# Dates for each chunk and each tile, written out as lists, in a planned kernel of attention and two mixtures

## The chip, the cores and the metric

The kernel runs on one core of a Trainium2 chip. The metric is the time of one execution on the device, in microseconds (us). Of three runs of the kernel before the median is 1030.25 us (1030.01 to 1031.8).

## The reference, cut to what matters

```python
# gated linear attention: 4 batches x 8 heads x 768 steps x 48
for t in range(S):
    state = alpha[:, :, t, :, None] * state + einsum('bhd,bhe->bhde', k[:, :, t], v[:, :, t])
    y[:, :, t] = einsum('bhd,bhde->bhe', q[:, :, t], state)
x = y.transpose(0, 2, 1, 3).reshape(3072, 384)

# first mixture, d_ff = 2048
h = x @ w_in
P = a[0] + a[1] * h + a[2] * h**2 + a[3] * h**3
Q = 1.0 + abs(b[0]) * abs(h) + abs(b[1]) * h**2
x = (P / (Q + 1e-06)) @ w_out

# second mixture, d_ff = 1536
g = x @ w_gate
out = (g * sigmoid(g) * (x @ w_val)) @ w_out
```

All arrays are float32 (weights may come as float64, which the kernel reads as pairs of words).

## The kernel before, in words

**Three stages.** Attention is worked in 24 chunks of 128 steps (`attention`, six for each batch): four transposes and products on TensorE, two scans and two products on VectorE (L669, L677, L685, L695), copies on ScalarE, masks on GpSimd. Its result goes through DRAM (`xd`) to the first mixture. The first mixture (`moe1`) works in six blocks of 512 tokens and 16 slices of 128 of d_ff; one slice of one block is a *tile*. A tile is nine multiplications into `h` (`mm1`), then a chain on ScalarE, GpSimd and VectorE that evaluates P / Q (L866 to L896, L880 and L807 on GpSimd, L881 to L892 on VectorE), and nine multiplications (`mm2`) into three accumulators `acc`. Every product is made of three, from values split into a rounded part and its rest. The second mixture (`moe2`) does the same with `pg`, `pv` and four accumulators `po`. Beside them every weight is brought in and split (`split`: ScalarE, VectorE, GpSimd), and in the end `bounds` reads alpha and the weights again and counts values out of range.

**Segments.** The spec given to `segments` cuts the first mixture into nine runs of tiles, each of one block: block 0, slices 0 to 5; block 1, 0 to 5; block 2, 0 to 5; block 3, all; block 0, 6 to 15; block 1, 6 to 15; block 2, 6 to 15; block 4, all; block 5, all. After the last tile of each, the three accumulators are emptied to `ys` (L921 on ScalarE, or, for the second part of a block, L927 on VectorE, added to what the first part left in DRAM), and `ys` is stored to `y1d`, from where the second mixture reads it. The next segment's `mm2` needs the accumulators' banks; there are three of them. Tiles of the next segment can run their `mm1` before that, as far as the other five banks and the four buffers of `gg` go.

**The planner.** `plan.op(v, how, reads, writes)` notes a step with a date v, its engine (or several, in order of preference) and a duration. `order` first works out when each step is due, from the last to the first:

```python
t = [due[u] - (dur + self.hop(e, ...) if full else 0.0) for u, full in users[i]]
if e == PE or not t:
    t.append(v)
due[i] = min(t)
...
due = [d - self.bias.get(g, 0.0) for d, g in zip(due, self.groups)]
```

`users` are the steps that depend on this one. So a step on TensorE is due at its own date or when its users need it; any other step goes by its users, and by its own date only if it has none. Then the planner goes through time with the durations it was given. Where an engine is free, it takes, of the steps that are ready on it, the one that is due first; it doesn't wait for a date. A step's second engine may be taken only from `due + late - THETA` on, where `late` is how far TensorE's last step was behind its due time. The order in which steps were picked is the order of the instructions in each engine's queue, and of the loads and stores in SP's queue.

**The dates.** `cv[m]` is the date of chunk m, whose steps on TensorE are dated up to 6 x 1.28 behind it. `vs` holds, for each segment, the date of each tile's `mm1`; its `mm2` is dated MM2 behind it. Before the change both come from formulas: a tile takes `step` (4.08), and the chunks' need is spread over the tiles at PA = 7.58 each. `vs2` are the dates of the second mixture's tiles, P2 apart; its `mm4` is dated 9.09 behind. The biases set the chunks ("att"), the weights ("w"), the loads of x ("x") and the tiles ("moe") against each other.

Of the kernel before, what the change touches and what calls it, by code (L numbers as in the profile page):

```python
# [19 lines left out]
PE, DVE, ACT, POOL, DMA = range(5)  # L20
CAPS = {"w": 99, "early": 9, "att": 3, "h": 5, "acc": 3, "po": 4, "g": 4, "tr": 1, "cv": 1}
HOP = {PE: 0.22, DVE: 0.2, ACT: 0.2, POOL: 0.15, DMA: 2.1}
SAME = {PE: 0.0, DVE: 0.07, ACT: 0.09, POOL: 0.05, DMA: 2.1}
THETA = 3.82


class Buf:
# [327 lines left out]
def gla_moe_moe2_kernel(  # L355
# [18 lines left out]
    NT, DM = out.shape  # L374
    F1 = w_in.shape[1] // 128
    F2 = w_gate.shape[1] // 128
    C = 128
# [6 lines left out]
    SIZES = [512,512,512,512,512,512]  # L384
    TMAX = max(SIZES)
    HEAD = [sum(SIZES[:n]) for n in range(len(SIZES) + 1)]
# [7 lines left out]
    plan = Plan()  # L394
# [68 lines left out]
    for nm in "akqv":  # L463
        for i in range(NBV if nm == "v" else 1):
            t = A.tile([128, H, 64], F32, name=f"nat{nm}{i}")
# [336 lines left out]
    def pool(T, f):  # L802
        return (POOL, 0.2 + T * 0.0021, f)
# [37 lines left out]
    def moe1(vs, n, part, f0, f1, xt, win, wout):  # L841
        acc = [bank("acc", f"acc{j}") for j in range(NJ)]

        T = SIZES[n]

        def first(f):
            v = vs[f - f0]
            hb = bank("h", "h")

            def h():  # L850
                return hb.t[:, 0:T]

            def cut(b):
                return lambda: b.t[:, 0:T]

            def mm1():
                for j in range(NJ):
                    s = slice(j * 128, (j + 1) * 128)
                    x = xt[j].t
                    mm3(h(), win[f].t[:, 0, s], win[f].t[:, 1, s], x[:, 0, 0:T], x[:, 1, 0:T], j == 0, j == NJ - 1)  # L860

            plan.op(v, [(PE, 9 * (T / 2400 + 0.0135), mm1)], (win[f], *xt, params), (hb,))
            b1, b2, b4 = (new("mp", [128, TMAX], F32, x, c) for x, c in (("t1", 3), ("t2", 2), ("t4", 3)))
            t1, t2, t4 = cut(b1), cut(b2), cut(b4)
            gg = new("mp", [128, 2, TMAX], F32R, "gg", LAG + 1)
            plan.op(v, [act(T, lambda: nc.scalar.activation(t1(), h(), AF.Abs), sb=False)], (hb,), (b1,))  # L866
            plan.op(
                v,
                [
                    act(T, lambda: nc.scalar.activation(  # L870
                        t2(), t1(), AF.Identity, scale=absb[:, 1:2], bias=absb[:, 0:1]), 2),
                    (POOL, 0.17 + T * 0.001, lambda: nc.gpsimd.tensor_scalar(
                        t2(), t1(), absb[:, 1:2], absb[:, 0:1], ALU.mult, ALU.add)),
                ],
                (b1,), (b2,),
            )
            plan.op(v, [act(T, lambda: nc.scalar.activation(t4(), h(), AF.Identity, scale=a3, bias=a2), 2, False)],
                    (hb,), (b4,))

            plan.op(v, [pool(T, lambda: nc.gpsimd.tensor_tensor(t1(), t1(), t2(), ALU.mult))], (b1, b2), (b1,))  # L880
            plan.op(v, [dve(T, lambda: nc.vector.tensor_tensor(t4(), t4(), h(), ALU.mult))], (b4, hb), (b4,))  # L881
            plan.op(v, [dve(T, lambda: nc.vector.scalar_tensor_tensor(t4(), t4(), a1, h(), ALU.add, ALU.mult), 1)],
                    (b4, hb), (b4,))
            plan.op(v, [act(T, lambda: nc.scalar.activation(t2(), t1(), AF.Ln, bias=oneps), 1)], (b1,), (b2,))
            last_exp[0] = plan.op(v, [act(T, lambda: nc.scalar.activation(h(), t2(), AF.Exp, scale=-1.0))], (b2,), (hb,))  # L885
            plan.op(v, [dve(T, lambda: nc.vector.scalar_tensor_tensor(t1(), t1(), ONE_EPS, h(), ALU.add, ALU.mult))],  # L886
                    (b1, hb), (b1,))
            plan.op(v, [dve(T, lambda: nc.vector.scalar_tensor_tensor(h(), t4(), a0, h(), ALU.add, ALU.mult), 1)],
                    (b4, hb), (hb,))
            plan.op(  # L890
                v,
                [dve(T, lambda: nc.vector.scalar_tensor_tensor(  # L892
                    t4(), t1(), 2.0, h(), ALU.subtract, ALU.mult, reverse0=True))],
                (b1, hb), (b4,),
            )
            plan.op(v, [act(T, lambda: nc.scalar.copy(gg.t[:, 0, 0:T], t4()))], (b4,), (gg,))  # L896
            plan.op(v, sub(T, lambda: gg.t[:, 1, 0:T], t4, lambda: gg.t[:, 0, 0:T])[:1], (b4, gg), (gg,))
            return gg

        def second(f, gg):  # L900
            def mm2():
                for j in range(NJ):
                    s = slice(j * 128, (j + 1) * 128)
                    w, g = wout[f].t, gg.t
                    mm3(acc[j].t[:, 0:T], w[:, 0, s], w[:, 1, s], g[:, 0, 0:T], g[:, 1, 0:T], f == f0, f == f1 - 1)

            plan.op(vs[f - f0] + MM2, [(PE, 9 * (T / 2400 + 0.0135), mm2)], (wout[f], gg), tuple(acc))

        pend = []
        for f in range(f0, f1):  # L910
            pend.append((f, first(f)))
            if len(pend) > LAG:
                second(*pend.pop(0))
        for z in pend:
            second(*z)
        vl = vs[-1] + MM2
        for j in range(NJ):
            ys = new("mp", [128, TMAX], F32, "ys", YS)
            yc = cut_(ys, T)
            if part == 0:  # L920
                how = [act(T, lambda j=j, yc=yc: nc.scalar.copy(yc(), acc[j].t[:, 0:T]), 0, False),  # L921
                       dve(T, lambda j=j, yc=yc: nc.vector.tensor_copy(yc(), acc[j].t[:, 0:T]))]
                plan.op(vl - 2.0, how, (acc[j],), (ys,))
            else:
                plan.op(vl - 8.0, [(DMA, 0.6 * T / 384, lambda j=j, yc=yc: nc.sync.dma_start(yc(), y1d[n].t[j]))],
                        (y1d[n],), (ys,))
                how = [dve(T, lambda j=j, yc=yc: nc.vector.tensor_tensor(yc(), yc(), acc[j].t[:, 0:T], ALU.add))]  # L927
                plan.op(vl - 2.0, how, (acc[j], ys), (ys,))
            plan.op(vl - 6.0, [(DMA, 0.6 * T / 384, lambda j=j, yc=yc: nc.sync.dma_start(y1d[n].t[j], yc()))],
                    (ys,), (y1d[n],))  # L930

# [97 lines left out]
    def moe2(vs, n, f0, f1, yy, wg, wv, wo):  # L1029
        po = [bank("po", f"po{t}") for t in range(CPB)]  # L1030
# [27 lines left out]
        def second(f, pp):  # L1058
            def mm4():
                for t in range(CPB):  # L1060
                    s = slice(t * 128, (t + 1) * 128)
                    o, w = po[t].t[:, 0:DM], wo[f].t
                    nc.tensor.matmul(o, pp.t[:, 0, s], w[:, 0], start=f == f0, stop=False)  # L1063
                    nc.tensor.matmul(o, pp.t[:, 0, s], w[:, 1], start=False, stop=False)  # L1064
                    nc.tensor.matmul(o, pp.t[:, 1, s], w[:, 0], start=False, stop=f == f1 - 1)  # L1065

            plan.op(vs[f - f0] + 9.09, [(PE, 2.09, mm4)], (wo[f], pp), tuple(po))

        pend = []
        for f in range(f0, f1):  # L1070
# [5 lines left out]
        vl = vs[-1] + 4.0  # L1076
# [26 lines left out]
            plan.op(vl, [(DMA, 0.6, lambda os=os, r0=r0: nc.sync.dma_start(out[r0 : r0 + 128, :], os.t))], (os,), ())  # L1103


    PA, P2 = 7.58, 6.18
    MM2 = 16.91

    def segments(nf, spec):

# [6 lines left out]
        return r  # L1117

    segs = segments(F1, "0:0-6 1:0-6 2:0-6 3 0:6-16 1:6-16 2:6-16 4 5")
    step = [18 * (SIZES[n] / 2400 + 0.0135) for n, _, _, _ in segs]  # L1120

    at, need = [0.0], []
    for (n, part, f0, f1), p in zip(segs, step):
        need.append((at[-1], HEAD[n + 1] // C if part == 0 else 0))
        at.append(at[-1] + p * (f1 - f0))
    s0 = 36.82
    LEADM = 53.00
    done = HEAD[1] / C
    cv = [3.50 + 6.65 * m for m in range(HEAD[1] // C)]
    start, vs = [], []  # L1130
    t, w = s0, 0.0
    for (n, part, f0, f1), p in zip(segs, step):
        start.append(t)
        row = []
        for f in range(f0, f1):
            row.append(t)
            rate = max([(k_ - done) / max(w_ - w - LEADM, p) for w_, k_ in need if w_ > w and k_ > done], default=0.0)
            c = min(rate * p, NT / C - done)
            while len(cv) < int(done + c + 1e-6):
                cv.append(max(t - 16.20, cv[-1] + 5.80))  # L1140
            done += c
            w += p
            t += p + PA * c
        vs.append(row)
    end_a = t
    i0 = len(plan.ops)
    plan.bias = {"w": -4.22, "att": 12.04, "x": 0.54, "moe": -2.25}
    plan.group = "att"
    for m in range(NT // C):
        if m == 1:  # L1150
# [13 lines left out]
    plan.group = None  # L1164

    segs2 = segments(F2, "0:0-2 1:0-2 2:0-2 0:2-6 1:2-6 2:2-6 0:6-12 1:6-12 2:6-12 3 4 5")
    t, vs2 = end_a + 16.75, []
    for n, part, f0, f1 in segs2:
        vs2.append([t + P2 * i for i in range(f1 - f0)])
        t += P2 * (f1 - f0)  # L1170
    wg, wv, wo = [], [], []
# [4 lines left out]
        wo.append(load_f(vw + 3.0, "wo", w_out2, f))  # L1176
    for (n, part, f0, f1), row in zip(segs2, vs2):
        moe2(row, n, f0, f1, load_y(row[0], n), wg, wv, wo)
    flag = bounds(end_a + 94.88, vs2[-1][0] - 20.0)

    for _, i, f in plan.order():
        for b in plan.ops[i][3]:
# [43 lines left out]
```

## Time and profile before

| | us |
|---|---|
| median of three runs (lowest, highest) | 1030.25 (1030.01, 1031.8) |
| the profiled execution | 1031.37 |
| its span, first to last instruction | 1029.7 |
| TensorE busy (matmul) | 993.9 |
| TensorE busy (weight load) | 836.6 |
| VectorE busy | 766.4 |
| ScalarE busy | 612.7 |
| GpSimd busy | 466.4 |

The mean granted clock of TensorE was 0.99. In the trace, PE is TensorE, PEld its loading of weights, DVE VectorE, ACT ScalarE, POOL GpSimd, SP the engine whose queue issues the loads and stores. In brackets at the end of a row of the timeline stands how long the engine had been idle before it, and what ended that. Names such as `h`, `acc`, `gg`, `ys`, `aT`, `pp` are those of the code. A matmul is shown with its time from entry to end; the next enters before that, so the pace of TensorE is read from the starts.

### The profile page before, as it was taken

To read this page: it belongs to the slowest core of one execution; us is meant where nothing else is said; L and a number is where in the kernel's file an instruction comes from. 1 tells how busy PE (TensorE), PEld (TensorE's weight loads), DVE (VectorE), ACT (ScalarE), POOL (GpSimd) and SP (SyncE) were. 2 spreads that over 40 slices of the span, in tenths; PEclk is the share of its full clock that TensorE was granted. 3 is DMA by queue.
4 is the path that set the end of the run, shared out by engine and by line. 5 is a ranking of instruction groups with operands and counts; after the bars stand their busy time and mean duration, and the time that the engine had idled before them with its cause. 6 is when DMAs were issued, how large, how long until landed. Compare 5 with 4: busy or idle time off the path is not lost.

```text
span 1029.7 us, 15684 instructions
## 1 busy us (share of the span) xinstructions
PE 993.9 (97%) x5542; PEld 836.6 (81%) x5542; DVE 766.4 (74%) x1442; ACT 612.7 (60%) x1120; POOL 466.4 (45%) x433
## 2 busy tenths in 40 slices
PE   8899999999999999999899999999999999999997
PEld 7777787778888788878678888888888888888886
DVE  6999988898869968797879784369876666666322
ACT  4676899899988868889989673222222112212111
POOL 2348887998856756666989883000000000000000
PEclk9999999999999999999989999999999999999999
DMA  7888754434322221220132661133653543543000
GB/s 169 202 194 203 194 140 131 131 101 108 93 72 54 90 63 48 71 91 1 32 108 77 195 204 47 46 108 108 192 175 110 183 122 114 154 123 96 28 1 34
DMA packets 159462, 113.56 MB, mean 110 GB/s; under 512 B 105232, under 2 KB 132880, under 8 KB 159376
## 3 DMA queue, kind: packets, MB, share of 16 engines
q1 hardware_dynamic: 159376, 112.49, 39.6%
q8 instruction: 45, 0.74, 0.3%
q14 instruction: 41, 0.34, 0.1%
HBM read 95.95 MB, written 16.52 MB: 109 GB/s over the span
## 4 chain that ended last, share of the span: by engine, by line
PE 46%; ACT 3%; DVE 2%; POOL 1%; issue 1%; DMA 0%; DVEq 0%; SPq 0%; POOLq 0%
PE pv L837 5%; PE pv L839 5%; PE pv L838 5%; PE pg L838 5%; PE pg L839 5%; PE po L1065 5%; PE po L1063 5%; PE po L1064 5%; PE pg L837 5%; PE acc L837 1%; PE acc L839 1%; PE acc L838 1%; PE h L837 1%; PE h L838 1%; PE h L839 1%
## 5 line engine op out<-in xcount | busy, mean ns | idle before, releaser
L880 POOL TENSOR_TENSOR t<-t,t 128x512 f32<-128x512 f32 x96 | 125.2, 1305 | 48.0 <-ACT t L870 41.0
L807 POOL TENSOR_TENSOR gg<-t,gg 128x512 fp32r<-128x512 f32 x96 | 128.8, 1343 | 39.7 <-ACT gg L896 21.9
L1046 ACT ACTIVATE sg<-pg 128x512 f32<-128x512 f32 x72 | 43.1, 598 | 170.7 <-PE pg L839 170.0
L1047 DVE TENSOR_TENSOR sg<-sg,pv 128x512 f32<-128x512 f32 x72 | 49.5, 687 | 126.5 <-PE pv L839 126.5
L837 PE MATMUL h<-xt,win 128*128 128x512 f32 x288 | 117.0, 406 | 13.5 <-DVE t L892 8.7
L1049 ACT CAST pp<-sg 128x512 fp32r<-128x512 f32 x72 | 44.8, 622 | 131.8 <-DVE sg L1047 118.9
L837 PE MATMUL acc<-gg,wout 128*128 128x512 f32 x288 | 115.5, 401 | 2.0 <-DVE t L892 2.0
L839 PE MATMUL h<-xt,win 128*128 128x512 f32 x288 | 114.0, 396 | 0.3 <-DVE win L530 0.3
L838 PE MATMUL h<-xt,win 128*128 128x512 f32 x288 | 114.0, 396 | 0.0
L838 PE MATMUL acc<-gg,wout 128*128 128x512 f32 x288 | 113.2, 393 | 0.3 <-POOL gg L807 0.2
L839 PE MATMUL acc<-gg,wout 128*128 128x512 f32 x288 | 112.7, 391 | 0.0
L886 DVE SCALAR_TENSOR_TENSOR t<-t,h 128x512 f32<-128x512 f32 x96 | 65.4, 683 | 46.9 <-ACT h L885 45.7
L1063 PE MATMUL po<-wo,pp 128*128 128x384 f32 x288 | 97.2, 337 | 0.7 <-ACT part L1087 0.7
L1065 PE MATMUL po<-wo,pp 128*128 128x384 f32 x288 | 97.2, 338 | 0.0
L1064 PE MATMUL po<-wo,pp 128*128 128x384 f32 x288 | 96.9, 337 | 0.0
L838 PE MATMUL pg<-yy,wg 128*128 128x512 f32 x216 | 85.1, 394 | 0.7 <-DVE yy L945 0.7
L837 PE MATMUL pv<-yy,wv 128*128 128x512 f32 x216 | 85.6, 396 | 0.0
L839 PE MATMUL pv<-yy,wv 128*128 128x512 f32 x216 | 85.4, 395 | 0.0
L838 PE MATMUL pv<-yy,wv 128*128 128x512 f32 x216 | 85.2, 395 | 0.0
L839 PE MATMUL pg<-yy,wg 128*128 128x512 f32 x216 | 85.2, 394 | 0.0
L837 PE MATMUL pg<-yy,wg 128*128 128x512 f32 x216 | 84.9, 393 | 0.0
L981 DVE TENSOR_SCALAR_CACHE_REDUCE chk_x<-chk_e 128x384 f32<-128x384 uint32 x136 | 75.1, 552 | 3.8
(143 smaller groups left out, 2492.2 us busy)
## 6 DMA issues: line engine op xcount, KB each, us to landing
chk<-in_moe_w_out_dram SPq DMA_DIRECT2D x28, 384.0 KB, 3.3
yr<-y1d SPq DMA_DIRECT2D x36, 256.0 KB, 2.7
xr<-xd SPq DMA_DIRECT2D x27, 256.0 KB, 2.8
y1d<-ys SPq DMA_DIRECT2D x27, 256.0 KB, 2.3
win_st<-in_moe_w_in_dram SPq DMA_DIRECT2D x16, 384.0 KB, 3.8
wout_st<-in_moe_w_out_dram SPq DMA_DIRECT2D x16, 384.0 KB, 3.8
chk<-in_moe_w_in_dram SPq DMA_DIRECT2D x16, 384.0 KB, 3.9
nata<-in_alpha_dram SPq DMA_DIRECT2D x24, 192.0 KB, 3.4
```

The lines of the kernel that those rows point to most:

```text
L807: return lambda: eng.tensor_tensor(out_(), in0(), in1().bitcast(F32), ALU.subtract)
L837: nc.tensor.matmul(out_, wh, xh, start=start, stop=False)
L838: nc.tensor.matmul(out_, wh, xl, start=False, stop=False)
L839: nc.tensor.matmul(out_, wl, xh, start=False, stop=stop)
L880: plan.op(v, [pool(T, lambda: nc.gpsimd.tensor_tensor(t1(), t1(), t2(), ALU.mult))], (b1, b2), (b1,))
L886: plan.op(v, [dve(T, lambda: nc.vector.scalar_tensor_tensor(t1(), t1(), ONE_EPS, h(), ALU.add, ALU.mult))], (b1, hb), (b1,))
L981: [(DVE, 0.4, lambda: nc.vector.tensor_scalar(dst(), src(), bound, 0.0, op_, ALU.add, accum_out=cnt.t[:, c : c + 1]))],
L1047: plan.op(v, [(DVE, 0.6, lambda: nc.vector.tensor_tensor(sg.t, sg.t, pv.t, ALU.mult))], (sg, pv), (sg,))
L1049: plan.op(v, [(ACT, 0.53, lambda: nc.scalar.copy(pp.t[:, 0], sg.t))], (sg,), (pp,))
L1063: nc.tensor.matmul(o, pp.t[:, 0, s], w[:, 0], start=f == f0, stop=False)
L1064: nc.tensor.matmul(o, pp.t[:, 0, s], w[:, 1], start=False, stop=False)
L1065: nc.tensor.matmul(o, pp.t[:, 1, s], w[:, 0], start=False, stop=f == f1 - 1)
```

## The change

The formulas for the dates of chunks and tiles go, and two lists stand in their place. THETA, three biases, P2, MM2, the second mixture's start, the dates of `mm4`, of the emptying copies and of the checks get other numbers. No step, no size and no buffer is changed.

```diff
-THETA = 3.82
+THETA = 3.39
...
-                plan.op(vl - 2.0, how, (acc[j],), (ys,))
+                plan.op(vl - EV, how, (acc[j],), (ys,))
...
-                plan.op(vl - 2.0, how, (acc[j], ys), (ys,))
+                plan.op(vl - EV, how, (acc[j], ys), (ys,))
...
-            plan.op(vs[f - f0] + 9.09, [(PE, 2.09, mm4)], (wo[f], pp), tuple(po))
+            plan.op(vs[f - f0] + 9.60, [(PE, 2.09, mm4)], (wo[f], pp), tuple(po))
...
-    PA, P2 = 7.58, 6.18
-    MM2 = 16.91
+    MM2 = 16.92
+    EV = 5.79
...
-    s0 = 36.82
-    LEADM = 53.00
-    done = HEAD[1] / C
-    cv = [3.50 + 6.65 * m for m in range(HEAD[1] // C)]
...
-            rate = max([(k_ - done) / max(w_ - w - LEADM, p) for w_, k_ in need if w_ > w and k_ > done], default=0.0)
-            c = min(rate * p, NT / C - done)
-            while len(cv) < int(done + c + 1e-6):
-                cv.append(max(t - 16.20, cv[-1] + 5.80))
-            done += c
-            w += p
-            t += p + PA * c
-        vs.append(row)
-    end_a = t
+    cv = [3.5, 10.6, 17.0, 27.5, 29.5, 33.6, 40.7, 46.8, 52.0, 54.8, 66.1, 64.2, 93.7, 105.3, 115.4, 125.5, 162.8, 209.7, 250.2, 293.5, 328.7, 371.3, 413.4, 460.2]
+    vs = [
+        [36.3, 100.0, 113.2, 124.8, 136.4, 148.0],
+        [152.2, 157.3, 163.9, 167.4, 172.5, 177.5],
+        [182.6, 187.7, 192.7, 197.3, 202.3, 201.8],
+        [212.5, 217.5, 222.6, 227.7, 232.7, 238.3, 243.3, 248.4, 253.5, 258.5, 263.6, 268.7, 272.3, 277.4, 282.5, 287.5],
+        [294.0, 299.0, 304.1, 308.5, 314.2, 319.3, 324.4, 336.1, 341.2, 346.2],
+        [351.3, 356.4, 361.4, 366.5, 365.7, 371.5, 376.6, 381.7, 386.8, 391.8],
+        [396.8, 401.9, 407.0, 409.9, 416.1, 421.2, 419.4, 426.6, 431.6, 433.9],
+        [441.0, 446.0, 451.1, 456.6, 460.3, 464.3, 469.3, 473.4, 477.5, 480.7, 484.8, 488.8, 492.9, 497.0, 501.1, 505.2],
+        [509.3, 513.3, 515.0, 523.5, 527.6, 531.7, 535.8, 539.8, 543.9, 549.8, 551.8, 555.6, 559.2, 561.9, 564.9, 569.4],
+    ]
+    P2 = 6.45
+    end_a = 585.14
...
-    plan.bias = {"w": -4.22, "att": 12.04, "x": 0.54, "moe": -2.25}
+    plan.bias = {"w": -3.37, "att": 12.90, "x": 0.25, "moe": -2.25}
...
-    t, vs2 = end_a + 16.75, []
+    t, vs2 = end_a + 5.14, []
...
-    flag = bounds(end_a + 94.88, vs2[-1][0] - 20.0)
+    flag = bounds(end_a + 103.59, vs2[-1][0] - 20.0)
```

## Rows read from the trace of the kernel before

**Rows 1.** The page, part 1: busy us, share of the span, instructions.

```profile
PE 993.9 (97%) x5542; PEld 836.6 (81%) x5542; DVE 766.4 (74%) x1442; ACT 612.7 (60%) x1120; POOL 466.4 (45%) x433
```

**Rows 2.** Busy us of each engine in stretches of the span.

```profile
core 0: us, PE busy (x) PEld busy (x) DVE busy (x) ACT busy (x) POOL busy (x), PEclk, DMA share, GB/s
60.00:80.00 20.00, 17.88 (x168) 14.11 (x167) 19.93 (x35) 16.45 (x35) 11.39 (x12) 1.00 0.77 177
...
280.00:300.00 20.00, 20.00 (x131) 16.19 (x129) 13.87 (x22) 16.96 (x31) 11.08 (x10) 1.00 0.25 73
...
380.00:400.00 20.00, 20.00 (x130) 16.37 (x129) 14.91 (x24) 17.07 (x31) 12.85 (x13) 1.00 0.36 107
...
680.00:740.00 60.00, 60.00 (x289) 52.23 (x288) 55.58 (x157) 13.88 (x23) 0.00 (x0) 1.00 0.53 160
```

**Rows 3.** TensorE's timeline at five changes of segment: start, us.

```profile
181.71 0.50 PE L837 MATMUL h<-xt,win 128*128 128x512 f32 x1 [2.65 <-ACT al L662]
...
183.22 0.60 PE L837 MATMUL h<-xt,win 128*128 128x512 f32 x1
...
186.66 0.40 PE L839 MATMUL acc<-gg,wout 128*128 128x512 f32 x1
...
211.58 0.50 PE L837 MATMUL h<-xt,win 128*128 128x512 f32 x1 [1.53 <-DVE qt L695]
...
346.93 0.69 PE L837 MATMUL h<-xt,win 128*128 128x512 f32 x1 [2.53 <-DVE t L892]
...
350.68 0.39 PE L837 MATMUL acc<-gg,wout 128*128 128x512 f32 x1
...
447.62 0.50 PE L837 MATMUL acc<-gg,wout 128*128 128x512 f32 x1 [2.02 <-DVE t L892]
...
517.23 0.80 PE L837 MATMUL h<-xt,win 128*128 128x512 f32 x1 [6.21 <-DVE t L892]
...
521.21 0.39 PE L837 MATMUL acc<-gg,wout 128*128 128x512 f32 x1
```

**Rows 4.** The timelines of GpSimd and TensorE at the last product of block 4.

```profile
496.67 1.30 POOL L807 TENSOR_TENSOR gg<-t,gg 128x512 fp32r<-128x512 f32 x1
...
498.29 0.39 PE L837 MATMUL h<-xt,win 128*128 128x512 f32 x1
...
500.33 0.39 PE L837 MATMUL acc<-gg,wout 128*128 128x512 f32 x1
```

**Rows 5.** ScalarE's timeline: block 4's accumulators are emptied.

```profile
516.57 1.10 ACT L921 COPY ys<-acc 128x512 f32<-128x512 f32 x2
...
518.00 0.64 ACT L921 COPY ys<-acc 128x512 f32<-128x512 f32 x1
```

**Rows 6.** Stretches at two changes of segment; columns as in rows 2.

```profile
432.00:445.00 13.00, 13.00 (x60) 10.74 (x59) 12.69 (x22) 12.97 (x24) 10.04 (x9) 1.00 0.39 123
502.00:510.60 8.60, 8.56 (x38) 6.79 (x37) 8.19 (x15) 8.60 (x17) 8.60 (x9) 1.00 0.16 49
510.60:517.20 6.60, 0.42 (x2) 0.00 (x0) 5.48 (x10) 6.60 (x13) 6.52 (x7) 0.78 0.18 58
```

**Rows 7.** Two lines' instructions: duration ns min/median/max, first and last start.

```profile
L872 POOL TENSOR_SCALAR t<-t,absb x16: 766/770/787, 99.9 to 518.3; 128x512 f32<-128x512 f32 x16
...
L807 DVE TENSOR_TENSOR xt<-xr,xt x8: 661/686/1181, 44.6 to 486.7; 128x512 fp32r<-128x512 f32 x8
```

**Rows 8.** VectorE's groups in 403 to 420: busy us, mean ns.

```profile
L669 DVE TENSOR_TENSOR_SCAN bb<-al,seed_f 128x516 f32<-128x516 f32 x1 | 1.2, 1226 | 0.0
L677 DVE TENSOR_TENSOR_SCAN cc<-al,seed_r 128x516 f32<-128x516 f32 x1 | 1.2, 1226 | 0.0
L695 DVE TENSOR_TENSOR qt<-qT,bb 128x512 f32<-128x512 f32 x1 | 0.7, 692 | 0.2 <-PE qT L654 0.2
...
L685 DVE TENSOR_TENSOR kt<-kT,cc 128x512 f32<-128x512 f32 x1 | 0.7, 682 | 0.0
```

**Rows 9.** VectorE's subtraction `pp` (all, and one), GpSimd beside it.

```profile
L1052 DVE TENSOR_TENSOR pp<-sg,pp x72: 677/691/1510, 571.2 to 1019.6; 128x512 fp32r<-128x512 f32 x72
...
578.92 1.50 DVE L1052 TENSOR_TENSOR pp<-sg,pp 128x512 fp32r<-128x512 f32 x1
...
578.73 1.14 POOL L586 TENSOR_TENSOR wg_x<-wg_x,wg_r 128x384 uint32<-128x384 uint32 x1 [0.27 <-ACT wg L583]
```

More of the change, by code (lines that the diff above doesn't have):

```diff
@@ L1119, in gla_moe_moe2_kernel @@
     segs = segments(F1, "0:0-6 1:0-6 2:0-6 3 0:6-16 1:6-16 2:6-16 4 5")
[L1120 to L1125, printed above, removed]
-    s0 = 36.82
-    LEADM = 53.00
-    done = HEAD[1] / C
-    cv = [3.50 + 6.65 * m for m in range(HEAD[1] // C)]
[L1130 to L1136, printed above, removed]
-            rate = max([(k_ - done) / max(w_ - w - LEADM, p) for w_, k_ in need if w_ > w and k_ > done], default=0.0)
-            c = min(rate * p, NT / C - done)
-            while len(cv) < int(done + c + 1e-6):
-                cv.append(max(t - 16.20, cv[-1] + 5.80))
-            done += c
-            w += p
-            t += p + PA * c
-        vs.append(row)
-    end_a = t
+    cv = [3.5, 10.6, 17.0, 27.5, 29.5, 33.6, 40.7, 46.8, 52.0, 54.8, 66.1, 64.2, 93.7, 105.3, 115.4, 125.5, 162.8, 209.7, 250.2, 293.5, 328.7, 371.3, 413.4, 460.2]
+    vs = [
[9 rows of a table added]
+    ]
+    P2 = 6.45
+    end_a = 585.14
     i0 = len(plan.ops)
-    plan.bias = {"w": -4.22, "att": 12.04, "x": 0.54, "moe": -2.25}
+    plan.bias = {"w": -3.37, "att": 12.90, "x": 0.25, "moe": -2.25}
     plan.group = "att"
```

## The prediction

> **What bounds the kernel now.** I read the page's busy table first, then the stretches of 20 us, then TensorE's waits, then the other engines around the longest of them. TensorE is busy for 97% of the span [rows 1], so only its lost time can be won back. The stretches say where that lies [rows 2]. In 680 to 740 us TensorE is busy for the whole 60 us, although VectorE has 55.58 us of work there: from about 620 us on, the second mixture runs at TensorE's pace, and no date can shorten it. In 60 to 80 us VectorE is full (19.93 of 20) and TensorE has 17.88. In 280 to 300 and 380 to 400 TensorE has 20.00.
>
> Between these lie the changes of segment. I number the nine entries of `segs` S1 to S9, so there are eight changes, S1|S2 to S8|S9. Five of them cost time [rows 3]; nine multiplications at full clock take 2.04 us, from 498.29 to 500.33 [rows 4]:
> - S8|S9: a wait of 6.21, and then the clock at half speed, 517.23 to 521.21 being 3.98 in place of 2.04: 8.15 us.
> - S5|S6: 2.53, and 346.93 to 350.68 is 3.75 in place of 2.04: 4.24 us.
> - S2|S3: 2.65, and eight multiplications from 183.22 to 186.66 take 3.44 in place of 1.81: 4.28 us.
> - S7|S8: 2.02 us, and S3|S4: 1.53 us, both with no loss of clock.
>
> Together 20.22 us. S4|S5 and S6|S7 lie in the stretches with 20.00 and cost nothing; S1|S2 I take as nothing too.
>
> What happens at such a change is to be seen at S8|S9. The last product into the old accumulators begins at 500.33 [rows 4], so they are complete by 502.4 (500.33 + 2.04). The three copies that empty them start at 516.57 (two, merged) and 518.00 [rows 5], 14 us later, and the next accumulation begins at 521.21 [rows 3]. In between ScalarE is busy without a gap (8.60 of 8.60, then 6.60 of 6.60), and GpSimd all but so (8.60, then 6.52) [rows 6]. The planner explains it: a step that isn't on TensorE gets its due time from its users alone, and an emptying copy is used, through its store to `y1d`, only by the second mixture and by the following segments' copies. It is therefore due later than nearly all else on its engine and waits for a free place.
>
> **The change part by part.**
> *EV, and MM2.* `vl - EV` in place of `vl - 2.0` moves nothing. The copy has users (its store), so the planner never reads its own date. The cause named above stays as it is. MM2 moves by 0.01. Both zero; if I misread the rule, the copies of S8|S9 could come up to 14 us earlier, and up to 8.15 us would go.
>
> *Mixture 2: P2, end_a, 9.60, the checks.* Its first date goes from 580.39 + 16.75 = 597.14 to 585.14 + 5.14 = 590.28, its step from 6.18 to 6.45. Dates only rank what is ready; TensorE has no free time there, so zero. The check loads start at 688.7 in place of 675.3 and are spread to 931.5 in place of 923.2. Their loads on SP's queue and their counts on VectorE are hidden by TensorE, which had 60 of 60 with VectorE at 55.58; 8.3 us later at the end stays far from the last product near 1023. Were that cover gone, a stretch as full as 680 to 740 would show it; I take zero.
>
> *THETA 3.82 to 3.39.* A second choice of engine is allowed 0.43 us later. What it decided in the trace are 16 of 96 steps on GpSimd (L872) and eight subtractions of x on VectorE [rows 7]. If the two L872 that lie in S8|S9's stretch went to ScalarE, which is full there, it would cost twice 0.77, 1.5 us; if fewer second choices spare GpSimd as much, it gains 1.5. I take zero between.
>
> *The first 160 us.* Chunks 9 and 11 to 15 are due 4 to 7 us earlier (their date change, and 0.86 from the bias), the tiles of S1 almost as before, the weights 0.85 to 2.4 us earlier. VectorE is full in 60 to 80 [rows 2] and its work is the same, so I take zero. A chunk's four loads (4 x 196,608 bytes, at the 177 GB/s of that stretch 4.4 us) now pass weight loads on SP's queue; a weight late by that could hold a tile up to 4.4 us, and a chunk earlier by it could save as much. Both ends stay in the range.
>
> *The changes of segment.* Here the dates move against each other (the old ones are what the formulas of before give; a step is due at its date less its group's bias, which is -2.25 for the tiles before and after).
> S8|S9: the fourth tile of S9 was dated 527.3, the last product of S8 511.0 + 16.91 = 527.9; now 523.5 and 505.2 + 16.92 = 522.1. Their order turns round. In the trace that tile runs at 498.29 and the product at 500.33, though its last input was complete at 497.97 (496.67 + 1.30) [rows 4]. So the accumulators can be complete 2.04 us earlier.
> S7|S8: the last four products of S7 are due 5.0 to 7.8 earlier, S8's tiles 5.8; chunk 23 was due at 445.8 - 12.04 = 433.8, 15 us ahead of S8's first tile (446.8 + 2.25 = 449.0), and is now due at 460.2 - 12.90 = 447.3, 4 us behind it (443.2).
> S5|S6: the last three tiles of S5 and first four of S6 are due 5.8 later, chunks 20 to 22 3.6 to 7.2 later, the rest of S6 not.
> S2|S3 and S3|S4: the last tile of S3 is due 7.0 earlier, chunk 16 5.4 earlier, chunks 17 and 18 1.0 later.
>
> What the planner makes of that can't be read off by hand. From below: all five losses stay. From above: all go, 20.2 us. I take what the eight rows themselves say of a change whose order is dealt anew: their mean, 20.22 / 8 = 2.5 us. All five costly ones are dealt anew: 5 x 2.5 = 12.6, which is 7.6 less. Of the three free ones I give two an even chance of being dealt anew (chunks 12 to 15 and 22 move by 4 to 7 us near them): + 2.5. Net 5.1 us.
>
> **Sum.** The profiled execution took 1031.37 us, 1.1 above the median of the runs shown (1030.25). It would become 1026.3, the median 1025.2.
>
> **The rivals.**
> *R1, no change.* Readiness, not rank, fixes the order where it matters, and the copies are last as before. For: ScalarE's full stretch [rows 6], and EV that does nothing. Against: at least one order turns round, with its input ready [rows 4]. 1030.2 us.
>
> *R2, slower.* Chunk 23 moves into S7|S8. In the trace its VectorE work lies in 403 to 420: two scans of 1.226 us, and two products of 0.69 and 0.68 [rows 8], 3.8 us in all. VectorE has 12.69 of 13.00 in 432 to 445 [rows 6]. There the work goes straight into the wait of 2.02, which becomes 5.8, and the clock then falls as at S8|S9 for another 1.9: + 5.8, 1036.0 us. It decides from the point at which the scans start behind some 428 us. Against it: the last products of S7 are due earlier too, so the accumulators may be empty before the scans come.
> On VectorE beside GpSimd the row shows a subtraction of 1.50 us at 578.92 against a median of 0.691, with a GpSimd step beginning at 578.73 [rows 9]. The Trainium skill (SBUF — State Buffer, Who interferes with whom) says that a VectorE step with both inputs in SBUF and a GpSimd step that reads SBUF exclude each other for a whole instruction; the row agrees. By it the two scans could each take 0.81 more where GpSimd is busy, and R2 would cost 7.4 in place of 5.8, 1037.7 us.
>
> *R3, most of it goes.* The new dates leave every change like S4|S5: the five lose at most a fifth of 20.2, 16 us less, 1014 us. For: two changes show that it can be. Against: the late copies stay.
>
> **How the numbers follow.** What a measurement can tell from no change here is about 0.2%, 2.1 us. My forecast (1019 to 1028) has 0.43, R3 0.12, R1 0.22, R2 0.23. Faster is the forecast and R3 but for a little that falls within 2.1 us: 0.54. The same: R1 with that, less its upper edge: 0.21. Slower: 0.25. The range goes from R3 to R2, 1014 to 1036.
>
> **What would show it.** Right: waits of TensorE after 160 us of 10 us or less in all in place of 14.9 (the five above), S8|S9 below 6 us, the last product of S8 ahead of S9's fourth tile, the stretch from 620 us on as long as before, and the emptying copies still some 10 us behind the last product. Wrong: a wait of over 5 us at another change of segment, chunk 23's scans behind 428 us with a wait on VectorE there, or copies that now follow the products at once (then EV does act).

## The result and the profile after

The changed kernel takes 1019.63 us (median of 4 runs, 1019.14 to 1019.89), the kernel before 1030.65 us (4 runs, 1030.01 to 1031.8). The ratio is 0.9891, with a 95% interval of 0.9874 to 0.9908: 11.0 us faster. The way was forecast, the size was not: 5.1 us had been. The profiled executions, 1031.37 before and 1019.14 after, differ by 12.2.

The page's part 1 of the changed kernel, which answers to [rows 1], has the same share of busy time in a shorter span (1017.4 us):

```profile
PE 989.4 (97%) x5542; PEld 833.9 (82%) x5542; DVE 768.3 (76%) x1442; ACT 613.3 (60%) x1121; POOL 472.9 (46%) x432
```

The stretches of [rows 2], after (PE, PEld, DVE, ACT, POOL busy; clock; DMA):

```profile
60.00:80.00 20.00, 18.02 (x132) 14.11 (x132) 18.73 (x30) 15.76 (x31) 13.19 (x13) 0.91 0.52 130
280.00:300.00 20.00, 20.00 (x96) 16.56 (x95) 16.95 (x27) 18.66 (x33) 12.92 (x11) 1.00 0.32 83
380.00:400.00 20.00, 20.00 (x118) 16.53 (x117) 16.96 (x27) 18.50 (x32) 13.90 (x13) 1.00 0.24 74
680.00:740.00 60.00, 60.00 (x285) 51.77 (x284) 45.88 (x124) 14.51 (x25) 0.00 (x0) 1.00 0.35 108
```

Where the time went is read best from three long stretches. First before:

```profile
0.00:160.00 160.00, 147.52 (x1365) 122.46 (x1366) 143.54 (x223) 117.29 (x240) 101.14 (x116) 0.99 0.78 184
160.00:620.00 460.00, 443.35 (x2253) 363.36 (x2252) 386.71 (x600) 398.70 (x718) 358.02 (x312) 0.99 0.32 92
620.00:1000.00 380.00, 380.00 (x1815) 330.43 (x1814) 229.53 (x609) 91.51 (x155) 7.22 (x7) 1.00 0.36 108
```

and after:

```profile
0.00:160.00 160.00, 143.04 (x1285) 117.97 (x1286) 140.98 (x220) 116.96 (x235) 103.78 (x115) 0.99 0.74 177
160.00:620.00 460.00, 456.08 (x2393) 376.30 (x2393) 396.21 (x613) 405.03 (x733) 367.75 (x317) 1.00 0.33 94
620.00:1000.00 380.00, 380.00 (x1815) 330.39 (x1814) 227.25 (x606) 88.52 (x149) 1.35 (x1) 1.00 0.36 108
```

The idle time of TensorE is the stretch less its busy time. Up to 160 us it rises from 12.48 to 16.96 (+4.5). From 160 to 620 it falls from 16.65 to 3.92 (-12.7). From 620 on it stays at zero. Half-speed stretches come on top; before, three of them lost 1.94 + 1.71 + 1.63 = 5.3 us [rows 3].

All of TensorE's waits behind 160 us, after (waiter, who ended it, us in total, times, longest), in place of the five in [rows 3]:

```profile
PE h L837 <- DVE t L892: 2.2, 2, 1.8
PE kn_ps L729 <- ACT aa L713: 0.7, 1, 0.7
PE h L837 <- ACT aa L713: 0.5, 1, 0.5
PE kn_ps L729 <- DVE t L892: 0.4, 1, 0.4
```

Of the five changes that had cost time, only S8|S9 still loses more than some 0.3 us; S1|S2 now loses a little (table below). TensorE's timeline at S8|S9, which answers to [rows 3] and [rows 4]:

```profile
492.21 0.39 PE L837 MATMUL acc<-gg,wout 128*128 128x512 f32 x1
...
494.25 0.39 PE L837 MATMUL h<-xt,win 128*128 128x512 f32 x1
...
506.45 0.50 PE L837 MATMUL h<-xt,win 128*128 128x512 f32 x1 [1.84 <-DVE t L892]
...
507.95 0.63 PE L837 MATMUL h<-xt,win 128*128 128x512 f32 x1
...
511.59 0.40 PE L837 MATMUL h<-xt,win 128*128 128x512 f32 x1
...
514.35 0.39 PE L837 MATMUL acc<-gg,wout 128*128 128x512 f32 x1
```

The last product of S8 (nine multiplications from 492.21 to 494.25) now stands ahead of S9's fourth tile (494.25), as forecast. The wait is 1.84, and nine multiplications from 507.95 to 511.59 take 3.64 in place of 2.04: 3.4 us lost, in place of 8.15.

The copies that empty the accumulators, on ScalarE after, at S2|S3 and at S8|S9; they answer to [rows 5]:

```profile
166.15 0.59 ACT L921 COPY ys<-acc 128x512 f32<-128x512 f32 x1
...
168.16 1.09 ACT L921 COPY ys<-acc 128x512 f32<-128x512 f32 x2
...
496.12 0.60 ACT L921 COPY ys<-acc 128x512 f32<-128x512 f32 x1
...
506.05 0.62 ACT L921 COPY ys<-acc 128x512 f32<-128x512 f32 x1
...
511.37 0.65 ACT L921 COPY ys<-acc 128x512 f32<-128x512 f32 x1
```

At S8|S9 the last one is still 17 us behind the last product (494.3). At S2|S3 the last (the second of the merged two) begins 3.4 us behind the product, which ended at 165.3; before, it began 16.3 behind. The whole picture, worked out from the starts in both traces: the time from the end of a segment's last product to the start of the next segment's first, and what TensorE did in it (a tile is 2.04 us; attention's steps by their usual pace, so the loss is good to some 0.3 us).

| | before: length, tiles, attention, lost | after: length, tiles, attention, lost |
|---|---|---|
| S1\|S2 | 5.4: 2, 1.3, 0 | 7.3: 1, 3.6, 1.6 |
| S2\|S3 | 16.1: 5, 2.2, 3.7 | 8.1: 2, 3.7, 0.3 |
| S3\|S4 | 14.5: 6, 0.4, 1.8 | 6.2: 2, 2.3, 0 |
| S4\|S5 | 2.4: 1, 0.4, 0 | 4.6: 2, 0.4, 0 |
| S5\|S6 | 19.9: 7, 0.9, 4.8 | 16.9: 6, 4.4, 0.3 |
| S6\|S7 | 14.6: 5, 4.4, 0 | 15.3: 6, 3.2, 0 |
| S7\|S8 | 12.2: 6, 0, 2.0 (just behind it) | 16.2: 6, 3.9, 0 |
| S8\|S9 | 18.8: 5, 0, 8.6 | 20.1: 8, 0, 3.8 |

So the loss went in two ways, as far as the traces tell. At S2|S3 and S3|S4 the copies come early (the last of S3's begins 4 us behind the product, 13 before) and the change is short. At S5|S6 and S7|S8 the copies (VectorE's, with a load from `y1d` each) are about as late as before, some 15 us, but a chunk of attention gives TensorE 4 us of other work in between. Of these four, S7|S8 alone has runs of its own below; for the other three the reading rests on the traces before and after. Four rows of TensorE's timeline at S7|S8 after show chunk 23 in the gap, the fifth is S8's first product:

```profile
423.01 0.60 PE L654 MATMUL qT<-ident,natq 128*128 128x128 f32 x4
...
425.60 1.16 PE L704 MATMUL sc<-qt,kt 48*128 48x128 f32 x16
...
431.00 1.09 PE L752 MATMUL yT<-aa,natv 128*64 128x128 f32 x16
...
432.02 1.16 PE L758 MATMUL yT<-qt,st_s 128*128 128x128 f32 x8
...
439.17 0.39 PE L837 MATMUL acc<-gg,wout 128*128 128x512 f32 x1
```

and VectorE's timeline has that chunk's scans [rows 8], now at 417 to 422, and the emptying steps of S7 behind them:

```profile
417.46 1.44 DVE L669 TENSOR_TENSOR_SCAN bb<-al,seed_f 128x516 f32<-128x516 f32 x1
...
420.57 1.23 DVE L677 TENSOR_TENSOR_SCAN cc<-al,seed_r 128x516 f32<-128x516 f32 x1
...
423.49 0.68 DVE L927 TENSOR_TENSOR ys<-ys,acc 128x512 f32<-128x512 f32 x1
...
429.34 0.68 DVE L927 TENSOR_TENSOR ys<-ys,acc 128x512 f32<-128x512 f32 x1
...
437.78 0.68 DVE L927 TENSOR_TENSOR ys<-ys,acc 128x512 f32<-128x512 f32 x1
```

### The profile page after: what moved, and what is told of

Its sections match the earlier page's. It is cut to its first block, busy times and chain, and to the rows that moved or that the text cites. A ratio compares the mean times of both kernels' runs of the same rounds, so it can differ in the third digit from the quotient of the medians.

```text
span 1017.4 us, 15684 instructions
## 1 busy us (share of the span) xinstructions
PE 989.4 (97%) x5542; PEld 833.9 (82%) x5542; DVE 768.3 (76%) x1442; ACT 613.3 (60%) x1121; POOL 472.9 (46%) x432
## 4 chain that ended last, share of the span: by engine, by line
PE 78%; DVE 10%; ACT 8%; issue 2%; POOL 1%; DMA 0%; SPq 0%; DVEq 0%; ACTq 0%; POOLq 0%
PE pv L837 5%; PE po L1065 5%; PE pv L839 5%; PE pv L838 5%; PE pg L839 5%; PE po L1063 5%; PE po L1064 5%; PE pg L838 5%; PE pg L837 5%; PE acc L837 5%; PE acc L839 5%; PE acc L838 5%; PE h L837 5%; PE h L839 4%; PE h L838 4%
## 5 line engine op out<-in xcount | busy, mean ns | idle before, releaser
L880 POOL TENSOR_TENSOR t<-t,t 128x512 f32<-128x512 f32 x96 | 127.8, 1332 | 49.6 <-ACT t L870 43.9
L1049 ACT CAST pp<-sg 128x512 fp32r<-128x512 f32 x72 | 44.7, 621 | 129.4 <-DVE sg L1047 121.2
L881 DVE TENSOR_TENSOR t<-t,h 128x512 f32<-128x512 f32 x96 | 65.4, 683 | 18.1 <-ACT t L877 17.1
```

The lines of the kernel that those rows point to most:

```text
L1049: plan.op(v, [(ACT, 0.53, lambda: nc.scalar.copy(pp.t[:, 0], sg.t))], (sg,), (pp,))
```

## The experiments

Two questions. To whom does the gain belong: to the parts, each at the place that it re-dates (theory P), or to the one order that comes out of all numbers together (theory L)? And by which mechanism does a change of segment lose its time: by the late copies (C, against G: full engines, of which the late copies are only a sign), and by TensorE having nothing to do meanwhile (F, against V: the recorded rival that a chunk in the change costs time there)? Each ratio is to the kernel before on the same chip. Differences from the changed kernel are to its 1019.6 us above, which was not measured again beside them; the kernel before had 1030.4 to 1030.7 each time.

**MM2 back by 0.01** (changed kernel)

```diff
-    MM2 = 16.92
+    MM2 = 16.91
```

> The changed kernel with MM2 at 16.91 again, 0.01 less, and nothing else. Theory P (the gain belongs to parts: each list clears the changes of segment that it re-dates): MM2 is worth nothing, 1019.6 us, within 2 us. Theory L (one order: a single pair of steps that change place deals all that comes behind anew, and the new numbers fit only together): if 0.01 turns a pair round, waits of TensorE of 2 us and more come back behind it and most of the 11 us is gone, 1026 to 1036 us.

Measured: 1030.29 us (10 runs), ratio 1.0000 (0.9990 to 1.0009): the whole gain is gone. The first pair of steps that stands the other way round is on GpSimd: the subtraction of an `xt` and a product of a tile's chain. GpSimd's timeline, first in the changed kernel, then with MM2 at 16.91:

```profile
127.19 1.28 POOL L807 TENSOR_TENSOR xt<-xr,xt 128x512 fp32r<-128x512 f32 x1 [0.56 <-ACT xt L825]
128.43 1.30 POOL L880 TENSOR_TENSOR t<-t,t 128x512 f32<-128x512 f32 x1
```

```profile
128.00 1.27 POOL L880 TENSOR_TENSOR t<-t,t 128x512 f32<-128x512 f32 x1
129.23 1.29 POOL L807 TENSOR_TENSOR xt<-xr,xt 128x512 fp32r<-128x512 f32 x1
```

The products of TensorE come in the same order up to 131 us. Then the changed kernel has, behind the scores of a chunk, the first product of S2:

```profile
130.72 1.16 PE L704 MATMUL sc<-qt,kt 48*128 48x128 f32 x16
131.81 0.50 PE L837 MATMUL acc<-gg,wout 128*128 128x512 f32 x1
```

and with MM2 at 16.91 it has another step of the chunk there:

```profile
132.05 1.16 PE L704 MATMUL sc<-qt,kt 48*128 48x128 f32 x16
133.14 0.66 PE L729 MATMUL kn_ps<-ident,kt 128*128 128x128 f32 x4
```

The third copy of S1, at 129.4 with its neighbour in the changed kernel, comes at 152.56 here (ScalarE's timeline), the first product of S2 at 151.0:

```profile
152.56 0.60 ACT L921 COPY ys<-acc 128x512 f32<-128x512 f32 x1
```

Its two first long stretches:

```profile
0.00:160.00 160.00, 139.87 (x1228) 115.34 (x1229) 141.23 (x220) 118.24 (x236) 100.89 (x111) 0.97 0.71 169
160.00:620.00 460.00, 451.01 (x2391) 370.68 (x2390) 390.50 (x603) 399.31 (x721) 353.09 (x303) 1.00 0.34 95
```

TensorE idles 20.1 us up to 160 (17.0 in the changed kernel) and 9.0 behind it (3.9). L holds, P falls. That the one pair on GpSimd is the whole of it no run on the chip shows, but the planner's code does: with that pair alone turned round, its last step begins at 1016.7 us, as it does with MM2 at 16.91; with MM2 at 16.91 and that pair held in its place, at 1003.1, as in the changed kernel.

**THETA back** (changed kernel)

```diff
-THETA = 3.39
+THETA = 3.82
```

> The changed kernel with THETA at 3.82 again. Theory P: within 1.5 us of 1019.6, since only the second choices of engine (16 steps on GpSimd) hang on it. Theory L: 8 us and more slower than 1019.6, with new waits at changes of segment.

Measured: 1033.17 us, ratio 1.0025 (1.0012 to 1.0038), 13.5 us over the changed kernel. L.

**The tiles' dates alone** (kernel before)

```diff
     end_a = t
+    vs = [
+        [36.3, 100.0, 113.2, 124.8, 136.4, 148.0],
...
+    ]
```

> The kernel before with the list of the tiles' dates alone (chunks, biases, THETA, second mixture as before). Theory P: the tiles' dates clear S5|S6 and S8|S9, where they move most, and some 6 to 10 of the 11 us come: 1020 to 1025. Theory L: no share of the gain is owed to this list, 1027 to 1040 us, with waits behind 160 us of 12 us and more in all.

Measured: 1029.47 us, ratio 1.0000 (0.9972 to 1.0028). No share of the gain; TensorE idles 17.3 us from 160 to 620. L.

**The chunks' dates alone** (kernel before)

```diff
     end_a = t
+    cv = [3.5, 10.6, 17.0, 27.5, 29.5, 33.6, 40.7, 46.8, 52.0, 54.8, 66.1, 64.2, 93.7, 105.3, 115.4, 125.5, 162.8, 209.7, 250.2, 293.5, 328.7, 371.3, 413.4, 460.2]
...
-    plan.bias = {"w": -4.22, "att": 12.04, "x": 0.54, "moe": -2.25}
+    plan.bias = {"w": -4.22, "att": 12.90, "x": 0.54, "moe": -2.25}
```

> The kernel before with the list of the chunks' dates and their bias of 12.90 alone. Theory P: chunks 16 to 23 clear S2|S3 and S7|S8, 1024 to 1028; the later attention of the first 160 us costs its 4.7 us here too. Theory L: no gain, slower than before by up to 20 us, 1028 to 1050.

Measured: 1048.96 us, ratio 1.0192 (1.0144 to 1.0240): 18 us slower than before. L.

**The second mixture's numbers alone** (kernel before)

```diff
-            plan.op(vs[f - f0] + 9.09, [(PE, 2.09, mm4)], (wo[f], pp), tuple(po))
+            plan.op(vs[f - f0] + 9.60, [(PE, 2.09, mm4)], (wo[f], pp), tuple(po))
...
-    PA, P2 = 7.58, 6.18
+    PA, P2 = 7.58, 6.45
...
-    end_a = t
+    end_a = 585.14
...
-    plan.bias = {"w": -4.22, "att": 12.04, "x": 0.54, "moe": -2.25}
+    plan.bias = {"w": -3.37, "att": 12.04, "x": 0.54, "moe": -2.25}
...
-    t, vs2 = end_a + 16.75, []
+    t, vs2 = end_a + 5.14, []
...
-    flag = bounds(end_a + 94.88, vs2[-1][0] - 20.0)
+    flag = bounds(end_a + 103.59, vs2[-1][0] - 20.0)
```

> The kernel before with the second mixture's numbers alone (its start, P2, the date of mm4, the checks, the weights' bias of -3.37). Theory P: the handover at 580 to 620 us loses its 1.8 us, 1028 to 1031. Theory L: the weights' bias turns pairs round from the first 100 us on, slower, 1032 to 1048.

Measured: 1048.12 us, ratio 1.0171 (1.0151 to 1.0191), 18 us slower. L. So none of the three parts that were tried alone (this, the chunks, the tiles) carries any of the gain, and without the new MM2 or the new THETA the rest carries none either. The loads' bias had no run of its own.

**S8's copies due at their place** (kernel before). The due time is set behind the backward pass, so that no other step's due time changes.

```diff
+        for i, d in self.own.items():
+            due[i] = min(due[i], d)
         eng, beg, end = [None] * n, [0.0] * n, [0.0] * n
...
-                plan.op(vl - 2.0, how, (acc[j],), (ys,))
+                i = plan.op(vl - 2.0, how, (acc[j],), (ys,))
+                if (n, part) in ((4, 0),):
+                    plan.own[i] = vl + 3.0
```

> The kernel before, in which the three copies that empty S8's accumulators, and they alone, are due 3 us behind the date of S8's last product (in place of what their users ask). All that is planned ahead of some 502 us keeps its place. Theory C (the loss at S8|S9 is the copies' late place on ScalarE): the copies start by 506, the loss of 8.15 there goes, and the time falls by 6 to 8 us, 1022 to 1025. Rival G (ScalarE and GpSimd are full there, and the copies are late because of it): the stall comes elsewhere behind 502 us, within 2 us of 1030.7.

Measured: 1021.57 us, ratio 0.9912 (0.9893 to 0.9931): 8.8 us, about what S8|S9 had lost. Up to 500 us the steps of TensorE keep their order. Then one of the three copies runs on ScalarE at 501.08 and the other two on VectorE, their second choice of engine, from 500.82 to 502.10; the first product of S9 starts at 501.75 (before: all three on ScalarE, the last at 518.00, and the product at 521.21 [rows 3, 5]). TensorE has no idle time, though ScalarE is as full as before (20.00 of 20, before 19.67). The timelines of ScalarE, of VectorE and of TensorE, and the stretch:

```profile
501.08 0.62 ACT L923 COPY ys<-acc 128x512 f32<-128x512 f32 x1
```

```profile
500.82 1.28 DVE L924 COPY ys<-acc 128x512 f32<-128x512 f32 x2
```

```profile
501.75 0.39 PE L839 MATMUL acc<-gg,wout 128*128 128x512 f32 x1
```

```profile
500.00:520.00 20.00, 20.00 (x90) 16.57 (x89) 18.78 (x33) 20.00 (x37) 17.82 (x16) 1.00 0.30 99
```

So the copies' place in the order was the cause at S8|S9: with ScalarE as full as before, the copies are done within 2.5 us of the product's end (499.7), and no stall of that size comes elsewhere. C, and G falls. The due time does two things, though: it brings a copy forward in ScalarE's queue, and it lets a copy go to VectorE earlier. What each is worth alone was not tried.

**The same in the changed kernel** (the same lines, behind `vl - EV`)

> The changed kernel with the same due time for S8's copies. Theory C: the loss of 3.8 us at 500 to 520 goes, 1015.5 to 1017. Rival G: within 1.5 us of 1019.6.

Measured: 1018.16 us (1016.50 to 1019.21), ratio to before 0.9879 (0.9861 to 0.9897). The stretch of 500 to 520 has 20.00 busy (18.16 in the changed kernel), so the loss there is gone, but the time gains 1.5 us of the 3 to 4 expected, and the intervals of the two kernels overlap. By its time alone the run lies in G's range; it is the trace that speaks for C. What took back the rest isn't settled; 1.2 us of it is a wait for the second mixture's inputs that comes up at 560 to 600 us.

**All nine segments' copies due at their place** (kernel before; the condition names all nine)

> The kernel before with the copies of all nine segments due 3 us behind the last product. If the late copies are the cause at each change and the rest keeps its place, up to 20 us go: 1010 to 1018. Theory L (one order, dealt anew from the first copy that moves, at 129 us): the gain at single changes is lost to others, 1022 to 1040.

Measured: 1030.03 us, ratio 0.9990 (0.9976 to 1.0004). The same remedy everywhere gains nothing. It moves copies from 129 us on, so the order behind is another one, with its own waits: 15.8 us of idle time from 160 to 620, almost the 16.65 of before. The trace shows where it went: TensorE's waits at the seven changes behind 160 us (up to the end of the next segment's first product) fall from 14.9 to 6.6 us, and those inside the segments rise from 1.6 to 9.1. L again.

**Chunk 23 early** (changed kernel)

```diff
-    cv = [3.5, 10.6, 17.0, 27.5, 29.5, 33.6, 40.7, 46.8, 52.0, 54.8, 66.1, 64.2, 93.7, 105.3, 115.4, 125.5, 162.8, 209.7, 250.2, 293.5, 328.7, 371.3, 413.4, 460.2]
+    cv = [3.5, 10.6, 17.0, 27.5, 29.5, 33.6, 40.7, 46.8, 52.0, 54.8, 66.1, 64.2, 93.7, 105.3, 115.4, 125.5, 162.8, 209.7, 250.2, 293.5, 328.7, 371.3, 413.4, 433.0]
```

> The changed kernel with chunk 23 dated 433.0 in place of 460.2, so that its 6 us on TensorE run ahead of S7|S8 (423 to 439 us) and no longer in it. All that is planned ahead of some 380 us keeps its place. Theory F (attention's work on TensorE fills the time in which the accumulators are emptied): a loss of 3 us and more comes back at S7|S8, with the wait and, if it is long, the clock, 1023 to 1029. Rival V (the recorded prediction's: the chunk's VectorE work in the change of segment costs time there): it gets better by 1 to 4 us, 1016 to 1019.

Measured: 1026.19 us (1025.86 to 1026.34), ratio 0.9951 (0.9934 to 0.9968): 6.6 us over the changed kernel. S7|S8 (430.5 to 445.6) has seven tiles and no attention in it; the products of its first tile wait, the last of them for a copy (`ys`), and the clock falls to half speed, a granted clock of 0.50 in 450.4 to 455.6 (TensorE's timeline):

```profile
448.59 0.50 PE L837 MATMUL acc<-gg,wout 128*128 128x512 f32 x1 [2.09 <-DVE t L892]
...
450.39 0.80 PE L837 MATMUL acc<-gg,wout 128*128 128x512 f32 x1 [0.51 <-DVE ys L927]
```

The stretch around it:

```profile
440.00:460.00 20.00, 16.77 (x59) 12.55 (x58) 13.69 (x23) 15.03 (x26) 11.53 (x10) 0.83 0.15 53
```

(20.00 busy and a clock of 1.00 in that stretch of the changed kernel.) F holds for this place, and V falls. The 6.6 us are not the price of this place alone: TensorE's order is a new one from 387 us on, and S6|S7 has four tiles in it now, not six.

**Chunk 23 late** (kernel before)

```diff
     end_a = t
+    cv[23] = 460.2
```

> The kernel before with chunk 23 alone dated 460.2 in place of 445.8. Theory F: the loss of 2.0 at S7|S8 goes, S8|S9 keeps its 8; 1027 to 1031, and the trace shows the chunk's products between the last product of S7 and the first of S8. Rival V: the wait at S7|S8 grows to 5 us and more, 1033 to 1037.

Measured: 1029.98 us, ratio 0.9996 (0.9984 to 1.0007). The chunk's products stand in S7|S8 and its wait of 2.02 is gone, as F has it. But waits of 0.94 and 0.74 come up earlier, at 422.11 and 430.84, in the tiles beside the chunk:

```profile
422.11 0.50 PE L837 MATMUL h<-xt,win 128*128 128x512 f32 x1 [0.94 <-DVE t L892]
...
430.84 0.50 PE L837 MATMUL h<-xt,win 128*128 128x512 f32 x1 [0.74 <-ACT aa L713]
```

So V has a grain of truth: the chunk isn't free beside the tiles. Here the two about cancel, and the time alone says nothing for F; it excludes V's 1033 to 1037.

**Other dates, with copies due at their place.** Two kernels with dates that differ from both kernels'. How these dates were found is not on record. The first is nearer to the changed one:

```diff
-THETA = 3.39
+THETA = 3.85
...
-    MM2 = 16.92
+    MM2 = 17.22
...
+    OWN = {(4, 0): 3.0, (1, 1): 3.0, (0, 1): 0.0, (1, 0): 99.0, (2, 0): 3.0, (3, 0): 6.0, (2, 1): 6.0, (0, 0): 10.0}
...
+    cv = [14.4, 29.9, -1.5, 16.0, 39.6, 25.6, 41.2, 59.3, 40.3, 91.7, 68.8, 56.7, 90.9, 130.4, 121.1, 120.3, 172.3, 209.8, 243.5, 298.5, 335.8, 363.5, 410.0, 451.0]
...
```

> The changed kernel with due times of their own for the copies of seven of the eight segments that have a successor, and with other dates for chunks and tiles, MM2 17.22, THETA 3.85 and other biases. By theories C and F together (copies that come early, attention in the rest of the change of segment) no loss at any change of segment is left, the first 160 us as before: 1012 to 1016.5. If the copies' due times cost elsewhere what they save, 1018 to 1024.

Measured: 1018.12 us (1016.34 to 1019.24), ratio 0.9881 (0.9864 to 0.9898). No change of segment loses time any more (at most some 0.4 us by the reckoning of the table), yet the time is not below that of the kernel with S8's copies alone: waits inside S4 (200 to 280 us) take their place. The first expectation was missed; the second, that the due times cost elsewhere what they save, fits, just inside its range.

The second has the copies' own date in the planner's rule (`if e == PE or not t or i in self.own`), and hardly a date in common with the changed kernel:

```diff
-THETA = 3.39
+THETA = 2.19
...
-    MM2 = 16.92
+    MM2 = 14.80
...
+    cv = [4.4, 23.8, 4.8, 41.6, 88.0, 35.1, 56.2, 77.3, 48.9, 102.4, 96.2, 65.6, 126.7, 113.1, 124.2, 106.2, 169.7, 177.5, 248.8, 315.8, 340.9, 347.8, 408.6, 439.0]
...
```

> As the run before it, but all nine segments' copies at their own date in the planner's rule itself (4.92 us behind the last product), and dates unlike either kernel's (chunks up to 60 us elsewhere, MM2 14.80, THETA 2.19). Theory L (the time belongs to the order that comes out, not to any of the dates): 1013 to 1018 though hardly a date is the changed kernel's. Theory P: without the changed kernel's dates its gain goes, 1025 and more.

Measured: 1017.74 us (1017.43 to 1019.83), ratio 0.9880 (0.9860 to 0.9899). It does at least as well with wholly other dates, as L has it, and P falls. Since the copies' rule is another one too, the run does not part the dates' share from the copies'; and it shows that other dates can do it, not that any would. TensorE's waits behind 160 us are

```profile
PE h L838 <- DVE xt L807: 0.9, 1, 0.9
PE h L837 <- ACT yo L767: 0.6, 1, 0.6
PE pg L838 <- DVE yy L945: 0.2, 1, 0.2
```

The three kernels at 1017.7 to 1018.2 can't be told from one another, and lie 1.5 to 1.9 us below the changed kernel, with intervals that overlap its own. What is left is the first 160 us, where all of them idle 15 to 17 us.

## Why the prediction was right or wrong

*The bound, and the second mixture.* Right. From 620 to 1000 us TensorE is busy for 380.00 us before and after. The end of the check loads was misreckoned (not 923.2 and 931.5: the last one is issued at 945.7 before and 956.6 after), which cost nothing. That the second mixture's numbers are worth zero holds for that stretch only: alone, with the weights' bias among them, they made the kernel 18 us slower, by what they turn round before it.

*EV.* Right by the code: with EV alone changed, the planner hands out the steps of the kernel before in the same order on every engine. No run on the chip has EV alone. The late copies did stay the cause of what is left, at S8|S9.

*MM2 and THETA at zero.* Wrong, and for a reason that goes beyond them. Each was priced by the steps that it touches. But in the changed kernel 0.01 of MM2 turned one pair of steps round on GpSimd at 127 us, and taking it back cost 10.7 us; taking THETA back cost 13.5. A date has no price of its own here; the order has.

*The first 160 us at zero, with 4.4 us to either side.* The idle time rose by 4.5, at the edge of the bound. It was not traced to one date. Waits for the split of a weight, the mechanism that the prediction named, are part of it: 2.1 us at 60.59 and 0.6 at 80.47, where before there was one of 0.3.

*The changes of segment.* This is the step that failed: "I take what the eight rows themselves say of a change whose order is dealt anew: their mean, 20.22 / 8 = 2.5 us." The five that lost 20.2 lose 3.4 now, 0.7 each and not 2.5. Of the three free ones S4|S5 and S6|S7 stay free; S1|S2 loses 1.6 by the table's reckoning, which is part of the first 160 us. So the five gave -16.8, where -7.6 had been reckoned, and nothing of the +2.5 for the free ones came behind 160 us. Together with the rest: +4.5 in the first 160 us, -1.4 for two waits of 0.7 in 580 to 620 that went, and some +1.7 for small waits that are new (the four rows of waits less the 1.84, and 0.3 before). That is -12.0, against 12.2 measured between the profiled executions.

As the price of just any new order the mean was not far off. The runs with one part of the change (1029.5, 1048.1 and 1049.0 us) and with all of it but one number (1030.3 and 1033.2) have none below 1029. Reckoned as in the table, but to the end of the next segment's first product, the eight changes lose some 16 to 32 us in these five traces, 2.8 each in the mean, against some 8 in all in the changed kernel. The changed kernel's order is better than such an order, and the profile of before could not tell that.

The planner could. "What the planner makes of that can't be read off by hand" is so, but the planner is plain Python and goes through time with its own durations, without the chip. Its last step begins at 1016.7 us in the kernel before and at 1003.1 in the changed kernel: 13.6 earlier, where 11.0 was measured. The other orders come out in their places too: MM2 back 1016.7, THETA back 1020.9, the tiles alone 1018.2, the second mixture alone 1030.3, the chunks alone 1033.3. The measured times lie 11 to 19 us above the planner's over all kernels here, so it gives the size of a large change, not of one of 2 us. That 1019.63 still falls inside the forecast's 1019 to 1028 is no merit of the mean of the rows.

*R2, chunk 23 in S7|S8.* The chunk's steps on TensorE moved into S7|S8 as foreseen, but its scans (417 to 422) ran ahead of the change and not behind 428, so the condition that R2 named did not come. What the chunk did was the opposite: its 4 us on TensorE filled the time in which VectorE emptied the accumulators. I had looked at the engine that was full and not at the one that was about to be idle. Dated early again, it comes with a kernel 6.6 us slower. *R3* came true behind 160 us (the five lose 3.4, less than a fifth of 20.2) and left out the first 160 us. That the order of S8's last product and S9's fourth tile turns round was right, but it did not bring the last copy nearer to the product (17.1 us behind, before 15.6). S9 had 11 tiles ahead of its first product in place of 9.

## What to carry to other kernels

Where a list of priorities makes the order of all engines, price a change of its numbers as a new order and not as a sum of parts: one pair turned round early was worth as much as the whole change here. If the program that makes the order can be run by itself, run it and read its own times; if not, keep a wide range. In the trace, look at each place where a resource changes hands (here three accumulators) for two things: how late the step that frees it stands in its engine's queue, and what the engine that is short has to do in the meantime. Both were worth 4 to 9 us at a single place, and a remedy applied at one late place, with all ahead of it left alone, gave 8.8 us where the same remedy everywhere, with the same dates, gave nothing.

## What the runs showed of the hardware

TensorE fell to half speed (1.2 GHz, a granted clock of 0.50 in 508.0 to 511.3) after a wait of only 1.84 us at S8|S9 of the changed kernel, which cost 1.6 us more, while after the wait of 2.02 us at S7|S8 before it had kept its full speed (2.4 GHz, a granted clock of 1.00 in 447.6 to 453.0) [rows 3]. Even the same wait in the same order did both: the 2.65 us at S2|S3 was followed by a granted clock of 0.50 in 183.3 to 186.6 before, and by 1.00 in the run with S8's copies. So a wait's own length did not decide that here, and the 1.63 us that the clock cost at S2|S3 is not there in each execution; what else decides was not tried.
